# Attention computed a whole batch ahead, with transposed scores packed next to W1

## The chip, the cores and the metric

One core of one Trainium2 chip. The time is the device time of one execution in microseconds (us); a kernel's number is the median of its runs. The profile's span runs from the first to the last instruction and is about 1.8 us shorter than that time. "Fast runs" are those not in a disturbed state; a single run of a one-core program has the state "unknown".

The engines go by the profile's names: PE does the matmuls (PEld its weight loads), DVE is the vector engine, ACT the scalar engine, POOL is GpSimd, and SP does nothing here but issue DMAs. A small q (SPq) marks an engine's queue. PSUM is the memory that matmuls write, in banks. A hole is a time in which PE stands idle.

## The reference

Cross attention between x (8 batches, 8 heads, 512 tokens, 64 wide) and a state of 32 rows per head, in both directions, and then a two-layer network with SiLU (512 to 2048 to 512) over the result:

```
scores  = x @ state^T / 8        ; a  = softmax(scores)  ; xread = a  @ state     # 512 rows per head
scores2 = state @ x^T / 8        ; a2 = softmax(scores2) ; sread = a2 @ x         # 32 rows per head
y = concat(xread, sread)         ; h = y @ w_in          ; out = (h * sigmoid(h)) @ w_out
```

## The kernel before

The kernel folds the state into the first weight: for each batch, W1 = state @ w_in (its own matrix for each batch), so the hidden layer is W1^T times the attention weights a. A batch is 32 first-layer matmuls (`h`, from W1 and the transposed weights aT) and 64 second-layer ones (`o`), all 128x128 by 128x512, and the attention of the next batch, n = b + 1, is done in between. A pair (tt, ft) counts the second-layer matmuls: token tile tt of 4, hidden tile ft of 16.

```
def load_x(b, ...):                 # 1 MB, from GpSimd's queue (POOL)
    nc.gpsimd.dma_start(x_f[b % 2]..., x[b]...)
def transpose_x(b):                 # x^T by one DMA transpose of 512 KB, from the SP queue
    nc.sync.dma_start_transpose(xT[b], x_nat[b])
def scores(b, hg): ...              # 8 matmuls 128x128 by 128x64, into one of four rotating PSUM banks
def exps(b, hg):   ...              # one exp of 128x512 on ACT
def norm(b, hg, ...): ...           # sum, reciprocal (DVE), multiply (hg 0 on POOL, hg 1 on DVE)
def transpose_a(b, hg):             # aT by one DMA transpose of 128 KB, from the SP queue
    nc.sync.dma_start_transpose(aT[b][:, hg], an[b, hg])
...
# in the loop over batches, tiles tt and hidden tiles ft; n = b + 1
if at == (0, NFT - lead):  scores(n, 0); scores(n, 1); exps(n, 0); exps(n, 1)
if at == (1, 0):
    for hg in range(2):
        norm(n, hg, ...); transpose_a(n, hg)
    for c in range(4):     cast_x(n + 1, nc.gpsimd, c, 1)     # four casts on POOL
    load_x(n + 2)
if at == (2, 4):           sread(n); W1 first half            # takes all four rotating banks
if at == (3, 4):           W1 second half
if at == (3, 8):           transpose_x(n + 1)
```

The softmax here doesn't subtract the row's maximum and nothing guards it: scores larger than these inputs give would overflow.

## Time and profile before

| | before |
|---|---|
| time, median of 3 runs (lowest to highest) | 218.76 us (218.46 to 219.66) |
| span of the profiled run | 217.0 us |
| PE busy | 208.1 us (96%) |
| ACT, DVE, POOL busy | 142.5, 78.5, 42.0 us |
| one steady batch | 22.92 us |

The matmul stream (PE) is the bound: no other engine is busy for more than 73% of a steady batch, so what counts is the work of PE and whether something that PE needs arrives late. The lines that show this are in the prediction (in brackets, how long the engine was idle before and what ended that). One more view belongs here, because the result turns on it: the order of events on POOL and in the SP queue at (1, 0) of the loop over batch 4 (start, length, engine, line, operation, operands; in brackets, how long the engine was idle before and what ended that). First POOL, then SP:

```profile
122.34 1.04 POOL L327 TENSOR_TENSOR an<-exp_nat,rc 128x512 bf16<-128x512 bf16 x1 [18.30 <-ACT exp_nat L313]
123.33 2.74 POOL L153 CAST x_nat<-x_f 128x512 bf16<-128x512 f32 x4
126.03 0.93 POOL L106 DMA_DIRECT2D x_f<-in_x_dram  x1
```

```profile
123.41 2.50 SPq L337 DMA_TRANSPOSE aT<-an  x2
```

The two transposes of the weights leave at 123.41 and, one issue later, about 124.7; the casts keep the load of the next x back until 126.03.

### The profile page before, as it was taken

How to read it: one execution, taken by the hardware profiler on the slowest of the kernel's cores; microseconds unless marked ns; L12 is line 12 of the kernel's file. 1: busy time of each engine (PE TensorE's matmuls, PEld its weight loads, DVE VectorE, ACT ScalarE, POOL GpSimd, SP SyncE). 2: the span in 40 equal slices, each digit the busy share in tenths (PEclk: the TensorE clock that was granted, in tenths of full speed). 3: DMA queues.
4: the chain of work that ended last, by engine and by line, in shares of the span. 5: the costliest groups of instructions: out<-in, count | busy, mean ns of one | idle time of the engine just before them, and what ended most of it. 6: DMA issues, size and time to landing. Idle time of an engine off the chain costs nothing.

```text
span 217.0 us, 3946 instructions
## 1 busy us (share of the span) xinstructions
PE 208.1 (96%) x1579; PEld 98.0 (45%) x1605; DVE 78.5 (36%) x176; ACT 142.5 (66%) x243; POOL 42.0 (19%) x65
## 2 busy tenths in 40 slices
PE   7799999999999999999999989999999999999993
PEld 2433344444444444444444434444444444466652
DVE  4733248354642263206420632245222735200011
ACT  3765678799387956696669847893879566634410
POOL 8582004301600080006100440015000100000000
PEclk9999999999999999999999999999999999999999
DMA  5999999701497038802890199113510321011112
GB/s 191 186 204 207 220 340 300 227 37 51 111 211 183 0 108 259 174 3 75 232 201 34 54 155 285 50 51 102 146 51 0 102 102 48 0 48 51 48 48 97
DMA packets 33522, 27.09 MB, mean 125 GB/s; under 512 B 21344, under 2 KB 27360, under 8 KB 33504
## 3 DMA queue, kind: packets, MB, share of 16 engines
q1 hardware_dynamic: 26384, 14.95, 26.1%
q0 software_dynamic: 6976, 11.83, 24.0%
q8 instruction: 12, 0.20, 0.4%
q10 hardware_dynamic: 144, 0.07, 0.1%
q14 instruction: 6, 0.05, 0.1%
HBM read 17.43 MB, written 8.91 MB: 121 GB/s over the span
## 4 chain that ended last, share of the span: by engine, by line
PE 82%; issue 10%; DVE 2%; DMA 2%; POOL 2%; SPq 1%; POOLq 0%
PE o L485 43%; PE h L445 23%; PE ps_w L412 4%; PE h L464 3%; DMA aT<-an 2%; PE ps_busy L159 2%; PE o_half L507 2%; PE ps_sc L299 2%; PE o_a L485 1%; PE ps_sr L364 1%; POOL an L327 1%; DVE W L153 1%; PE ps_xt L245 1%; PE ps_at L344 1%; SPq L337 1%
## 5 line engine op out<-in xcount | busy, mean ns | idle before, releaser
L485 PE MATMUL o<-w_out_sb,g 128*128 128x512 bf16 x494 | 132.8, 380 | 1.9 <-issue 1.1
L477 ACT ACTIVATE g<-h 128x512 bf16<-128x512 f32 (+1 forms) x145 | 82.1, 571 | 35.7 <-PE h L445 21.4
L485 PEld LDWEIGHTS <-g 128*128 128x128 bf16 x528 | 49.8, 98 | 60.1 <-issue 7.0
L445 PE MATMUL h<-aT,W 128*128 128x512 bf16 x250 | 74.5, 379 | 0.7 <-DMA aT<-an 0.4
L153 DVE COPY o_sb<-o 128x512 f32<-128x512 f32 x17 | 11.6, 690 | 82.6 <-PE o L485 82.6
L445 PEld LDWEIGHTS <-W 128*128 128x128 bf16 x256 | 24.7, 97 | 31.3 <-issue 1.8
L153 DVE CAST W<-ps_w 128x512 bf16<-128x512 f32 (+1 forms) x31 | 20.5, 679 | 34.8 <-PE ps_w L412 34.8
L327 POOL TENSOR_TENSOR an<-exp_nat,rc 128x512 bf16<-128x512 bf16 (+1 forms) x9 | 9.1, 1014 | 112.2 <-DVE rc L325 56.7
L151 ACT ACTIVATE W<-ps_w 128x512 bf16<-128x512 f32 (+1 forms) x35 | 18.7, 577 | 7.6 <-PE ps_w L412 7.5
L151 ACT ACTIVATE o_sb<-o 128x512 f32<-128x512 f32 x15 | 8.9, 596 | 18.7 <-issue 9.1
L153 POOL CAST x_nat<-x_f 128x512 bf16<-128x512 f32 x24 | 16.0, 702 | 0.0
L412 PE MATMUL ps_w<-w_in_sb,stT 64*32 64x512 bf16 (+1 forms) x264 | 11.5, 376 | 0.0
L324 DVE TENSOR_REDUCE rs<-exp_nat 128x16 f32<-128x512 bf16 (+1 forms) x17 | 10.7, 630 | 1.4 <-ACT exp_nat L313 0.5
L106 POOL DMA_DIRECT2D x_f<-in_x_dram x8 | 7.0, 886 | 14.4 <-DVE x_rows L153 12.5
L313 ACT ACTIVATE exp_nat<-ps_sc 128x512 bf16<-128x512 f32 (+1 forms) x17 | 9.0, 570 | 1.3 <-PE ps_sc L299 1.2
L464 PE MATMUL h<-xmT,w_in_sb 128*128 128x256 bf16 x64 | 9.6, 273 | 0.1
L464 PEld LDWEIGHTS <-w_in_sb 128*128 128x128 bf16 x64 | 6.3, 98 | 3.9
L313 ACT ACT_TABLE_LOAD x6 | 7.7, 1283 | 0.1
L636 ACT ACT_TABLE_LOAD x6 | 7.7, 1283 | 0.1
L159 PE MATMUL ps_busy<-busy 128*128 128x512 bf16 x15 | 5.7, 497 | 1.4 <-DVE warm L166 1.2
L327 DVE TENSOR_TENSOR an<-exp_nat,rc 128x512 bf16<-128x512 bf16 (+1 forms) x8 | 6.7, 831 | 0.3
L299 PEld LDWEIGHTS <-xT 128*128 128x128 bf16 x128 | 4.9, 98 | 2.9 <-DVE xT L153 1.0
(59 smaller groups left out, 90.1 us busy)
## 6 DMA issues: line engine op xcount, KB each, us to landing
out_dram<-o_sb SPq DMA_DIRECT2D x33, 256.0 KB, 2.5
x_f<-in_x_dram POOLq DMA_DIRECT2D x6, 1024.0 KB, 7.9
w_in_sb<-in_moe_w_in_dram POOLq DMA_DIRECT2D x3, 512.0 KB, 10.1
w_out_sb<-in_moe_w_out_dram POOLq DMA_DIRECT2D x3, 512.0 KB, 11.8
x_f<-in_x_dram SPq DMA_DIRECT2D x2, 512.0 KB, 4.8
x_f<-in_x_dram POOLq DMA_DIRECT2D x2, 512.0 KB, 16.6
w_in_sb<-in_moe_w_in_dram POOLq DMA_DIRECT2D x2, 256.0 KB, 7.5
w_out_sb<-in_moe_w_out_dram POOLq DMA_DIRECT2D x2, 256.0 KB, 7.9
```

Source lines behind the costliest of these rows:

```text
L151: nc.scalar.activation(dst, src, func=COPY, bias=0.0)
L153: eng.tensor_copy(dst, src)
L159: nc.tensor.matmul(ps[:], busy[:, 0:128], busy[:], start=True, stop=True, skip_group_check=True)
L299: nc.tensor.matmul(sc_ps[hg][-1][:, c % m, ds(2 * j, 2), :], xT[b][:, c, 2 * hg + j, :], stT[:, b, 2 * hg + j, :, :], start=True, stop=Tru ...
L313: nc.scalar.activation(e[:, ds(n * i, n)], ps[:], func=EXP, bias=0.0, scale=SCALE)
L324: nc.vector.tensor_reduce(rs[:, ds(c, nr)], e[:, ds(c, nr)], axis=AX, op=ADD)
L327: eng.tensor_tensor(a[:, ds(c, n)], e[:, ds(c, n)], rc[:, ds(c, n)].to_broadcast([128, n, 4, NS]), op=MULT,)
L412: nc.tensor.matmul(pss[f, hg][ds(32 * s, 32), 0:n], stT[ds(r, 64), b, h // 2, s % 2, :], w_in_sb[ds(r, 64), h // 2, ds(f, n)], start=True, ...
L445: nc.tensor.matmul(h_ps[k][:], W1[b][:, hg, ds(128 * ft, 128)], aT[b][:, hg, :, :], start=(hg == 0), stop=(hg == 1), skip_group_check=True,)
L464: nc.tensor.matmul(ps[:, 0:256], w_in_sb[:, kt, ds(128 * ft, 128)], xmT[:, :, kt].rearrange("p t n b -> p t (n b)"), start=(kt == 0), stop ...
L477: nc.scalar.activation(g[:, ds(i, m)], ps[:, ds(i, m)], func=SILU, bias=0.0)
L485: nc.tensor.matmul(outs[tt][:], gt[b * NFT + ft][:, ds(128 * tt, 128)], w_out_sb[:, ft, :], start=(ft == 0), stop=(ft == NFT - 1), skip_gr ...
```

## The change

Its intent: from batch 3 on, the attention of batch m = b + 2 is done while batch b's network runs, so that its long chain (exp, transpose, normalize, transpose) has a whole batch of slack. Scores are computed transposed, in the 64x32 tile group that W1 already uses, next to W1's matmuls and without a mode switch of their own; the exponentials and their normalized form are each transposed by one DMA. Batch 2 still goes the old way, so the loop over batch 1 does both. The core of the diff (warm-up activations, PSUM tags and the old branch are cut; they do not matter here):

```
+    def scores_t(b):
+        scT_ps[0] = psO.tile(..., tag="o1");  scT_ps[1] = psH.tile(..., tag="h1")
+        for s in range(4):
+            for hg in range(2):                       # 8 matmuls, 64x32 tiles, 512 columns
+                nc.tensor.matmul(scT_ps[hg][ds(32 * s, 32), :], stT[ds(r, 64), b, h // 2, s % 2, :],
+                                 xT[b][ds(r, 64), :, h // 2, :], ..., tile_position=(r, 32 * s))
+    def exps_t(b):   # two exps on ACT, then one DMA transpose e <- eT of 256 KB
+    def norm_t(b):   # sum, reciprocal, multiply, then one DMA transpose aT <- a of 256 KB
 ...
             pe_transpose_a(1, 1, nc.vector)
-            for c in range(4):
-                cast_x(2, nc.gpsimd, c, 1)
+            for i in (2, 3):
+                for c in range(4):
+                    cast_x(i, nc.gpsimd, c, 1)        # batch 3's casts moved ahead
 ...
                     if at == (1, 0):                  # (for b == 1)
                         for hg in range(2):
-                            norm(n, hg, ...); transpose_a(n, hg)
-                        if n + 1 < B:
-                            for c in range(4):
-                                cast_x(n + 1, nc.gpsimd, c, 1)
-                        if n + 2 < B:
-                            load_x(n + 2)
+                            norm(2, hg, ...); transpose_a(2, hg)
+                        load_x(4)                     # now directly behind norm
+                if b == 2 and at == (0, 4):
+                    transpose_x(4)
 ...
+                if n < B and at == (1, 4):            # was (2, 4)
+                    scores_t(m)
+                    pss = w1_mms(n, ...)
+                    sread((0, 1, 2) if b == 1 else (n,))
+                    exps_t(m)
 ...
+                    if at == (3, 0):
+                        norm_t(m)
+                        if b == 1:
+                            for c in range(4):
+                                cast_x(4, nc.gpsimd, c, 1)
+                        if m + 2 < B:
+                            load_x(m + 2)
 ...
+                    if at == (2, 8):                  # was (3, 4)
                         w1_chunks(n, (2, 3), both)
 ...
-        copy(nc.vector, o[:], ps[:, 0 : DM // 2])     # last copy of all
+        for i, eng in enumerate((nc.vector, nc.scalar)):
+            copy(eng, o[:, ds(DM // 4 * i, DM // 4)], ps[:, ds(DM // 4 * i, DM // 4)])
```

More of the change, by code (lines that the diff above doesn't have):

```diff
@@ L61 @@
     wpool = ctx.enter_context(tc.tile_pool(name="wpool", bufs=2))
+    tpool = ctx.enter_context(tc.tile_pool(name="tpool", bufs=2))
+    e2pool = ctx.enter_context(tc.tile_pool(name="e2pool", bufs=3))
     gpool = ctx.enter_context(tc.tile_pool(name="gpool", bufs=28))
     opool = ctx.enter_context(tc.tile_pool(name="opool", bufs=4))
-    psO = ctx.enter_context(tc.tile_pool(name="psO", bufs=2, space=bass.MemoryType.PSUM))
+    psO = ctx.enter_context(tc.tile_pool(name="psO", bufs=1, space=bass.MemoryType.PSUM))
     psH = ctx.enter_context(tc.tile_pool(name="psH", bufs=2, space=bass.MemoryType.PSUM))
@@ L120, in padded, with spread_x @@
         )[:, :, :, 0:128]
+    def spread_x(b):
+        copy(nc.vector, padded(b), x_nat[b][:])
     def cast_x(b, eng, c0=0, nc_=4, h0=0, nh=H):
@@ L170 @@
     )
-    nc.scalar.activation(warm[:], warm[:], func=EXP, bias=0.0)
+    nc.scalar.activation(warm[:], busy[:, 0:1], func=EXP, bias=0.0)
     for hg in range(2):
@@ L259 @@
     cast_x(0, nc.scalar, 2, 2, 0, 4)
-    new_o = lambda sh, dt, nm: psO.tile(sh, dt, tag="o", name=nm)
+    o_tags = ["o0", "o1"]
+    new_o = lambda sh, dt, nm: psO.tile(sh, dt, tag=o_tags.pop(), name=nm)
     cast_x(0, nc.scalar, 2, 2, 4, 4)
@@ L313, in exps @@
             nc.scalar.activation(e[:, ds(n * i, n)], ps[:], func=EXP, bias=0.0, scale=SCALE)
+    scT_ps = {}
+    eT = {}
+    def scores_t(b):
+        scT_ps[0] = psO.tile([128, 512], FP32, tag="o1", name="ps_scT")
+        scT_ps[1] = psH.tile([128, 512], FP32, tag="h1", name="ps_scT")
+        for s in range(4):
+            for hg in range(2):
+                h = HEAD_OF_SLOT[hg][s]
+                r = 64 * (h % 2)
+                nc.tensor.matmul(
+                    scT_ps[hg][ds(32 * s, 32), :],
+                    stT[ds(r, 64), b, h // 2, s % 2, :],
+                    xT[b][ds(r, 64), :, h // 2, :],
+                    start=True,
+                    stop=True,
+                    tile_position=(r, 32 * s),
+                    skip_group_check=True,
+                )
+    def exps_t(b):
+        t = tpool.tile([128, 2, 512], BF16, tag="eT", name="eT")
+        e = e2pool.tile([128, 2, 4, 4, NS], BF16, tag="e2", name="e2")
+        for hg in range(2):
+            nc.scalar.activation(t[:, hg], scT_ps[hg][:], func=EXP, bias=0.0, scale=SCALE)
+            exp_nat[b, hg] = e[:, hg]
+        nc.sync.dma_start_transpose(
+            e.rearrange("p g c s n -> p (g c) (s n)"), t.rearrange("q g t -> q (g t)")
+        )
+        e2[b] = e
+    e2 = {}
+    def norm_t(b):
+        rs = att.tile([128, 2, 4, 4, 1], FP32, tag="rs2", name="rs2")
+        rc = att.tile([128, 2, 4, 4, 1], FP32, tag="rcn", name="rcn")
+        a = tpool.tile([128, 2, 4, 4, NS], BF16, tag="an2", name="an2")
+        nc.vector.tensor_reduce(rs[:], e2[b][:], axis=AX, op=ADD)
+        nc.vector.reciprocal(rc[:], rs[:])
+        for hg, eng in enumerate((nc.gpsimd, nc.vector)):
+            eng.tensor_tensor(
+                a[:, hg], e2[b][:, hg], rc[:, hg].to_broadcast([128, 4, 4, NS]), op=MULT
+            )
+        aT[b] = att.tile([128, 2, 4, 128], BF16, tag="aT", name="aT")
+        nc.sync.dma_start_transpose(
+            aT[b].rearrange("q g c p -> q (g c) p"), a.rearrange("p g c s n -> p (g c s n)")
+        )
     an = {}
@@ L483, in G2 @@
             else:
-                outs[tt] = psO.tile([128, DM], FP32, tag="o", name="o")
+                i = (tt + (b > 0)) % 2 if tt < 3 else 0
+                outs[tt] = psO.tile([128, DM], FP32, tag=f"o{i}", name="o")
         nc.tensor.matmul(
@@ L538 @@
     w1_cols(0, [(0, 256)], (nc.scalar, nc.scalar))
-    nc.scalar.activation(warm[:], warm[:], func=SILU, bias=0.0)
+    nc.scalar.activation(warm[:], busy[:, 0:1], func=SILU, bias=0.0)
     load_w_in(1024)
@@ L549 @@
         ones_beside_x(i, nc.gpsimd)
-    keep_busy(4, psO, "o")
+    keep_busy(4, psO, "o0")
     pe_transpose_a(0, 0, nc.vector)
-    keep_busy(1, psO, "o")
+    keep_busy(1, psO, "o0")
     pe_transpose_a(0, 1, nc.vector)
@@ L577 @@
         if ft == 14:
-            nc.scalar.activation(warm[:], warm[:], func=EXP, bias=0.0)
+            nc.scalar.activation(warm[:], busy[:, 0:1], func=EXP, bias=0.0)
             pe_transpose_x(1, 0, 1, engs=(nc.vector,))
@@ L596 @@
     store(0, 2, nc.scalar)
-    nc.scalar.activation(warm[:], warm[:], func=SILU, bias=0.0)
+    nc.scalar.activation(warm[:], busy[:, 0:1], func=SILU, bias=0.0)
     store(0, 1, nc.vector)
@@ L617 @@
         n = b + 1
+        m = n + 1
         lead = 4 if b == 1 else 6
@@ L623 @@
                     upto(NFT * b + min(lead + ft, NFT))
-                if b == 1 and at == (0, 1):
-                    transpose_state()
-                    for u in range(2):
-                        evict_state(u, nc.vector)
                 if b == B - 1 and at in ((0, 4), (0, 8)):
                     place_xm(at[1] // 8, nc.vector)
-                if n < B:
-                    if at == (0, NFT - lead):
-                        scores(n, 0)
-                        scores(n, 1)
-                        exps(n, 0)
-                        exps(n, 1)
-                        nc.scalar.activation(warm[:], warm[:], func=SILU, bias=0.0)
+                if b == 1:
+                    if at == (0, 1):
+                        transpose_x(3)
+                        transpose_state()
+                        for u in range(2):
+                            evict_state(u, nc.vector)
+                    if at == (0, 4):
+                        spread_x(2)
+                    if at == (0, NFT - lead):
+                        for hg in range(2):
+                            scores(2, hg)
+                        for hg in range(2):
+                            exps(2, hg)
@@ L637 @@
                     if at == (1, 0):
                         for hg in range(2):
-                            norm(n, hg, (((nc.gpsimd, nc.vector)[hg], 0, 4),))
-                            transpose_a(n, hg)
-                        if n + 1 < B:
-                            for c in range(4):
-                                cast_x(n + 1, nc.gpsimd, c, 1)
-                        if n + 2 < B:
-                            load_x(n + 2)
-                    if at == (3, 8):
-                        if n + 1 < B:
-                            transpose_x(n + 1)
@@ L649 @@
-                    if at == (0, 4):
-                        copy(nc.vector, padded(n), x_nat[n][:])
-                    if at == (2, 4):
-                        if b == 1:
-                            sread((0, 1))
-                        sread((n,))
-                        pss = w1_mms(n, [(0, 512), (512, 512)])
-                        w1_out(n, [(0, 512)], both, pss)
-                        for m in (0, 1, 2) if b == 1 else (n,):
-                            sread_out(m)
-                        w1_out(n, [(512, 512)], both, pss)
@@ L660 @@
-                    if at == (3, 4):
+                            norm(2, hg, (((nc.gpsimd, nc.vector)[hg], 0, 4),))
+                            transpose_a(2, hg)
+                        load_x(4)
+                elif at == (0, NFT - lead) and m < B:
+                    nc.scalar.activation(warm[:], busy[:, 0:1], func=EXP, bias=0.0)
+                if b == 2 and at == (0, 4):
+                    transpose_x(4)
+                if b > 1 and m + 1 < B:
+                    if at == (1, 0):
+                        for c in range(4):
+                            cast_x(m + 1, nc.gpsimd, c, 1)
+                    if at == (2, 10):
+                        transpose_x(m + 1)
@@ new lines @@
+                if n < B and at == (1, 4):
+                    if m < B:
+                        scores_t(m)
+                    pss = w1_mms(n, [(0, 512), (512, 512)])
+                    sread((0, 1, 2) if b == 1 else (n,))
+                    if m < B:
+                        exps_t(m)
+                        nc.scalar.activation(warm[:], busy[:, 0:1], func=SILU, bias=0.0)
+                    w1_out(n, [(0, 512)], both, pss)
+                    for i in (0, 1, 2) if b == 1 else (n,):
+                        sread_out(i)
+                    w1_out(n, [(512, 512)], both, pss)
@@ L661 @@
+                if m < B:
+                    if at == (2, 0):
+                        spread_x(m)
+                    if at == (3, 0):
+                        norm_t(m)
+                        if b == 1:
+                            for c in range(4):
+                                cast_x(4, nc.gpsimd, c, 1)
+                        if m + 2 < B:
+                            load_x(m + 2)
+                if n < B:
+                    if at == (2, 8):
                         w1_chunks(n, (2, 3), both)
```

## The prediction

> **What bounds the kernel now.** I read the page's busy shares first, then the stretches of one batch each, then the instructions in order of time inside one batch, and last the chain of waits at the two places where a batch was longer than its neighbours.
>
> ```profile
> PE 208.1 (96%) x1579; PEld 98.0 (45%) x1605; DVE 78.5 (36%) x176; ACT 142.5 (66%) x243; POOL 42.0 (19%) x65
> PEclk9999999999999999999999999999999999999999
> ...
> 73.24:96.15 22.91, 22.65 (x173) 10.26 (x176) 8.04 (x17) 16.66 (x28) 4.61 (x6) 1.00 0.51 129
> 96.15:119.10 22.95, 22.65 (x173) 10.26 (x176) 8.03 (x17) 16.70 (x28) 4.61 (x6) 1.00 0.54 128
> 119.10:142.54 23.44, 22.81 (x173) 10.24 (x176) 8.03 (x17) 16.62 (x28) 4.61 (x6) 1.00 0.53 126
> 142.54:165.46 22.92, 22.65 (x173) 10.26 (x176) 8.03 (x17) 16.67 (x28) 3.73 (x5) 1.00 0.29 83
> 165.46:187.90 22.44, 22.18 (x158) 9.77 (x160) 10.42 (x24) 16.24 (x27) 1.05 (x1) 1.00 0.19 61
> ```
>
> The first column after the stretch is its length, then the busy time of PE, PEld, DVE, ACT and POOL. PE is busy in 22.65 of about 22.92 us at full clock; nothing else passes 73%. So the kernel ends when the matmul stream ends, and only two things can change its time: the work in that stream, and holes in it. Each stretch begins right after the scores of a batch. The last one contains no scores, as there is no batch 8, and is 22.92 - 22.44 = 0.48 us shorter: a direct reading of what one batch's scores cost end to end. One stretch, 119.10 to 142.54, is 0.52 us longer than the others.
>
> The order in time of one batch (start, length, line, operands, count):
>
> ```profile
> 141.91 0.63 PE L299 MATMUL ps_sc<-stT,xT 128*128 128x64 bf16 x16
> 142.59 5.56 PE L485 MATMUL o<-w_out_sb,g 128*128 128x512 bf16 x25
> 148.08 0.43 PE L364 MATMUL ps_sr<-x_rows,exp_nat 128*32 128x65 bf16 x32
> 148.44 0.62 PE L412 MATMUL ps_w<-w_in_sb,stT 64*32 64x512 bf16 x16
> 149.23 2.75 PE L485 MATMUL o<-w_out_sb,g 128*128 128x512 bf16 x12 [0.16 <-issue]
> ...
> 153.42 0.63 PE L412 MATMUL ps_w<-w_in_sb,stT 64*32 64x512 bf16 x16
> 153.98 0.39 PE L485 MATMUL o<-w_out_sb,g 128*128 128x512 bf16 x1
> ```
>
> The program has 26 second-layer matmuls between scores and state read but 25 records, so one is missing just ahead of 142.59; the scores took 0.47 us, as the chain of waits also says (PE ps_sc x16, 0.47). The state read takes 148.44 - 148.08 = 0.36 us, W1's 16 matmuls 153.98 - 153.42 = 0.56 us. With pairs of full matmuls at 0.43 us in the chain (0.216 each), a batch is 96 x 0.216 = 20.7, scores 0.47, state read with W1 and the switch ahead of them 1.01, second W1 group with its switch 0.65: 22.83 of 22.92. There is no unused tenth in this loop.
>
> Two more readings, both used below:
>
> ```profile
> 28.49 0.41 PE L412 MATMUL ps_w<-w_in_sb,stT 64*32 64x512 bf16 x8
> 28.83 0.61 PE L485 MATMUL o<-w_out_sb,g 128*128 128x512 bf16 x2
> ...
> 50.97 0.69 DVE L153 COPY o_sb<-o 128x512 f32<-128x512 f32 x1 [4.69 <-PE o L485]
> 51.55 1.08 ACT L313 ACTIVATE exp_nat<-ps_sc 128x512 bf16<-128x512 f32 x2
> ...
> 128.34 0.38 PE L445 MATMUL h<-aT,W 128*128 128x512 bf16 x1
> ...
> 129.12 0.38 PE L445 MATMUL h<-aT,W 128*128 128x512 bf16 x1 [0.41 <-DMA aT<-an]
> ```
>
> Eight matmuls in the 64x32 grouping take 28.83 - 28.49 = 0.34 us, sixteen 0.56: eight more, inside a group that is there anyway, cost 0.22. And the long stretch is the one where the transposed attention weights landed late: 129.12 - 128.34 less one matmul of 0.22 is 0.56.
>
> **What the Trainium skill says.** "TensorE: Matmul & The Clock Gate", section "Wait — 56ns, not 53.3ns?", gives 215.7 ns from start to start at 512 columns; the trace's 0.43 us per pair agrees. "TensorEngine Tiling (Array Packing)", section "Key Properties", says that a change of tiling mode drains the array, while tiles of one mode run independently. The trace agrees: about 0.09 us of lost start time ahead of 153.42 (153.11 plus one matmul is 153.33), and the 0.34 and 0.56 above. "ScalarE: Activation LUTs", section "What ACT_TABLE_LOAD costs", gives about 1283 ns for a load; the rows here show 1283. "DMA: Bandwidth & Descriptors", section "Rules for kernel authors", advises to issue a DMA early and wait late; that is the intent of this change, and the 4.4 us of the one late transpose, against a median of 2.3, shows what too short a lead costs.
>
> **The change part by part.**
>
> Scores removed: batches 3 to 7 lose sixteen 128x64 matmuls with as many weight loads of 98 ns. 5 x 0.47 = 2.35 us off the stream.
>
> Transposed scores added: eight 64x512 matmuls for each of these batches, placed next to W1 in the same mode, so no new switch. 5 x 0.22 = 1.10 us on the stream. The state read moves behind W1, which leaves the number of switches as it was. I take that as nothing. Net -1.25.
>
> Exp and normalization: two exps of 128x512 as before (0.60 each), the same sum, reciprocal and multiply work on DVE and POOL in one piece. One more DMA transpose of 256 KB per batch; by the 2.3 us of 128 KB and the median 5.6 us of 512 KB I estimate 3.4 us for it. From the exps to the first use of the attention weights there is now a whole batch, some 30 us, against a chain of about 0.2 + 1.2 + 3.4 + 2.6 + 3.4 = 11 us. So the wait at 129 goes: -0.52. Table loads fall from six pairs in the loop to five; ACT is at 73%, so they are worth nothing.
>
> PSUM: the transposed scores borrow a bank of the second layer's output and one of the hidden pair. The first is free when DVE has copied the first output tile. The copy ended 1.1 us after that tile's last matmul began (143.45 to 144.56), and the new scores would start 1.2 us after it: just free, at most 0.1 us lost. The other is free since all hidden tiles are activated by then.
>
> Batch 1's loop, the transition, carries both methods. The exps of batch 2 still end at 52.63. W1 of batch 2 now comes four second-layer matmuls into the second token tile, at about 51.95 after the new scores, and takes all four rotating banks. Two of them hold batch 2's scores until its exps end. The first eight matmuls go (to 52.2), the rest wait until about 52.7: +0.5 us. Then DVE has batch 2's norm (to 54.9 as before), a W1 copy 0.7, three state-read outputs of 0.93 each and another W1 copy, which ends near 59.1; the second W1 group, now eight matmuls into the third token tile at 58.4, needs that bank half way through: another +0.45. Together +0.95 us, once.
>
> Tail: the last copy of 128x256 (0.42 on DVE) is shared. From 424 at 256 and 690 ns at 512 columns, 128 columns are about 0.29: -0.13.
>
> Sum: -2.35 + 1.10 - 0.52 + 0.95 - 0.13 = -0.95 us, so 218.76 becomes 217.8.
>
> **The rivals.** *No transition loss*: bank order or DVE order is kinder than I count, and the gain is the whole 1.9 us: 216.9. For it: both waits are half a microsecond on chains that I added up by hand. *A late transpose*: batch 4's x loads only after batch 2's norm (about 55.3), lands some 8 us later, is cast by POOL for 2.7 us behind batch 3's multiply, and its transpose is behind the last store of batch 1 in the SP queue, so it leaves near 68.8 and lands 3.8 to 7.3 us later; its scores want it near 75.9. Mostly in time; at worst 0.5 to 1 us more: 218.8. *Transposes in the way*: one DMA transpose more per batch delays stores on the same queue until output buffers run out. Against it: DMA is at about half in these stretches and the queue has roughly 12 of 22.7 us of issuing to do. If it came, each batch would lose up to 1 us and the time would be 221 or more. *A gain beyond 2%* would need 4.4 us; all scores of these five batches are 2.35, so nothing in the profile can give it.
>
> **Range and chances.** The sure terms are the scores (-1.25) and the late weights (-0.5); the unsure one is the transition (0 to +1.5, perhaps with batch 4's lateness). Repeats of the kernel before differ by 1.2 us (218.46 to 219.66). I give 217.8, 8 in 10 between 216.4 and 219.2; faster by over 2% 0.02, within 2% 0.95, slower by over 2% 0.03.
>
> **What would show it.** Stretches of steady batches should be 22.6 to 22.7 us. The eight new matmuls and W1's sixteen together should take about 0.78 us before the state read, against 0.56 for W1. No matmul should wait on aT from batch 3 on. In batch 1's loop PE should show one hole near 52 us ended by ACT's exp and one near 59 ended by a DVE copy of W. I am wrong if steady stretches stay at 22.9 (then a mode switch or the borrowed bank costs what the scores gave), or if holes ended by DMA or POOL appear.

## The result, and the profile after

The changed kernel is slower: median 222.06 us (221.42 to 222.58, 4 runs) against 218.87 us for the kernel before in the same rounds, ratio 1.014 (95% interval 1.0097 to 1.0183). It is within 2% and well outside my range of 216.4 to 219.2. A ratio is the mean time of one kernel's fast runs over the mean of the other's of the same rounds, so it is not quite the ratio of the medians. The profiled run took 222.43 us, span 220.7 us: 3.7 us more than the span before.

The steady loop did what it should. The page's first line and the stretches, cut right behind the state read of each batch (columns as in the prediction: length, then busy time of PE, PEld, DVE, ACT, POOL):

```profile
PE 207.1 (94%) x1539; PEld 96.5 (44%) x1565; DVE 75.7 (34%) x166; ACT 140.8 (64%) x246; POOL 42.2 (19%) x65
```

```profile
49.84:81.95 32.11, 26.79 (x299) 12.07 (x300) 13.23 (x33) 20.45 (x34) 8.84 (x12) 1.00 0.72 152
81.95:104.57 22.62, 22.36 (x165) 9.91 (x168) 7.52 (x16) 16.75 (x29) 4.70 (x6) 1.00 0.61 139
104.57:127.19 22.62, 22.36 (x165) 9.92 (x168) 7.59 (x16) 16.75 (x29) 4.70 (x6) 1.00 0.64 141
127.19:149.81 22.62, 22.36 (x165) 9.93 (x168) 7.58 (x16) 16.75 (x29) 1.49 (x1) 1.00 0.42 96
149.81:172.22 22.41, 22.14 (x158) 9.80 (x161) 7.60 (x16) 15.02 (x27) 1.50 (x1) 1.00 0.28 69
```

Three equal batches of 22.62 us, where they were 22.92 and once 23.44. The last one has no transposed scores in it, and is 22.62 - 22.41 = 0.21 us shorter: that is what they cost. But in the first stretch, 49.84 to 81.95, PE is idle for 32.11 - 26.79 = 5.3 us. The matmuls there, in order of time:

```profile
51.66 0.41 PE L331 MATMUL ps_scT<-xT,stT 64*32 64x512 bf16 x8
51.89 1.14 PE L466 MATMUL ps_w<-w_in_sb,stT 64*32 64x512 bf16 x16
52.96 0.96 PE L418 MATMUL ps_sr<-x_rows,exp_nat 128*32 128x65 bf16 x96
...
58.93 0.41 PE L466 MATMUL ps_w<-w_in_sb,stT 64*32 64x512 bf16 x8 [0.25 <-DVE W L158]
59.27 2.12 PE L540 MATMUL o<-w_out_sb,g 128*128 128x512 bf16 x9
64.10 0.60 PE L499 MATMUL h<-aT,W 128*128 128x512 bf16 x2 [2.71 <-DMA aT<-an]
...
80.59 0.41 PE L331 MATMUL ps_scT<-xT,stT 64*32 64x512 bf16 x8 [1.82 <-DMA xT<-x_nat]
80.81 0.61 PE L466 MATMUL ps_w<-w_in_sb,stT 64*32 64x512 bf16 x16
81.36 0.43 PE L418 MATMUL ps_sr<-x_rows,e 128*32 128x65 bf16 x32
```

The two large holes are named in the brackets: 2.71 us for the transposed weights of batch 2 (hole 1), and 1.82 us for the transposed x of batch 4 (hole 2). Both are DMA transposes that were issued early enough and landed late. The queues at the two places, first POOL, then SP:

```profile
54.25 0.93 POOL L108 DMA_DIRECT2D x_f<-in_x_dram  x1
...
68.39 2.27 POOL L158 CAST x_nat<-x_f 128x512 bf16<-128x512 f32 x4
70.62 0.93 POOL L108 DMA_DIRECT2D x_f<-in_x_dram  x1
```

```profile
54.34 3.23 SPq L391 DMA_TRANSPOSE aT<-an  x2
...
71.29 6.27 SPq L143 DMA_TRANSPOSE xT<-x_nat  x1
```

Each late transpose leaves within 0.7 us of a load of 1 MB. Batch 3's casts are no longer between `norm` and the load, so the load starts with the weights' transposes and not 2.6 us after them. At the second place one event releases both: the end of batch 4's casts at 70.66 frees POOL for the next load and lets the transpose of what was just cast go, behind one store. Hence theory A: **a load from another queue that starts together with DMA transposes holds them back until it has landed itself.** The rival, theory B: the transposes that the change adds (of the exponentials, and the state reads' earlier ones) delay one another on the SP queue, and the load is innocent.

The packets of the trace support A before any experiment. Per microsecond of the changed kernel, on the clock of the lines above, the KB that were started and the mean and longest time of one packet, transposes (SP queue, packets of 256 bytes) against the load (POOL queue, 4096 bytes):

```
us        transposes: KB, mean / longest ns      load: KB, mean / longest ns
56         64.8,   26 /  546                      60,  2494 / 2967
57          1.2,   18 /   18                      24,   452 / 1912
58          1.5,   19 /   22                      64,  1074 / 2015
59          3.2,   19 /   22                      36,   757 / 1285
60          9.8,  168 / 2946                     240,   188 /  198
61          0                                    300,   188 /  193
62         11.0,   18 /   21                     300,   188 /  193
63        245.5,   20 /   79                       0
```

(The row of 60 contains two transpose packets of 2946 ns. By 57, 121 KB of the two transposes' 256 KB had started.) From 57 to 60 hardly anything moves in either queue: many load packets take one to three microseconds, not 0.19. Then the load runs at full speed, and only when it is through (its last packet ends at 62.97) do the transposes go on, with the usual 20 ns per packet. At hole 2 the picture is alike but not as sharp: from 72 to 77 the transpose starts 0 to 13 KB per microsecond, then 99 and 123 KB beside the load's last packets.

The kernel before has such collisions too, at transposes for which nobody waits: that of the state read (`xs`) took 7.4, 7.8 and 6.1 us to landing where a load of x was under way (issued at 81.26, 104.17 and 128.07), and 2.3 us where none was (150.57). Its one long batch is another matter. There the second transpose of the weights took 4.4 us; but the load left 1.3 us behind it, as in the three batches before, where that transpose took 2.3 to 2.4 us. Its slow packets, up to 1979 ns, start at 126.4, and the load's first packet only at 127.7. What this batch alone has in these microseconds is a packet of 16 KB in the queue that the profile calls `instruction`, from 125.82 on, 1776 ns long. So it is not shown that the load made this transpose late, and the `instruction` packet is a suspect.

### The profile page after: what moved, and what is told of

It reads as the page before. It is cut to its first block, busy times and chain, and to the rows that moved or that the text cites.

```text
span 220.7 us, 3845 instructions
## 1 busy us (share of the span) xinstructions
PE 207.1 (94%) x1539; PEld 96.5 (44%) x1565; DVE 75.7 (34%) x166; ACT 140.8 (64%) x246; POOL 42.2 (19%) x65
## 4 chain that ended last, share of the span: by engine, by line
PE 78%; DMA 13%; POOL 2%; DVE 2%; issue 1%; ACT 1%; SPq 0%; POOLq 0%
PE o L540 44%; PE h L499 22%; DMA w_in_sb<-in_moe_w_in_dram 5%; DMA aT<-an 4%; DMA xT<-x_nat 4%; PE ps_w L466 4%; PE h L518 3%; PE o_half L562 2%; PE o_a L540 1%; DVE W L158 1%; PE ps_sr L418 1%; POOL w_in_sb L149 1%; PE ps_scT L331 1%; POOL w_out_sb L152 1%; ACT L319 1%
## 5 line engine op out<-in xcount | busy, mean ns | idle before, releaser
L499 PE MATMUL h<-aT,W 128*128 128x512 bf16 x244 | 73.1, 379 | 3.0 <-DMA aT<-an 2.7
L158 DVE CAST W<-ps_w 128x512 bf16<-128x512 f32 (+1 forms) x31 | 20.5, 677 | 29.1 <-PE ps_w L466 29.1
L361 POOL TENSOR_TENSOR an<-e,rcn 128x512 bf16<-128x512 bf16 x5 | 7.6, 1523 | 59.5 <-DVE rcn L359 59.5
L158 POOL CAST x_nat<-x_f 128x512 bf16<-128x512 f32 x24 | 13.7, 606 | 25.8 <-DMA x_f<-in_x_dram 25.8
L466 PE MATMUL ps_w<-w_in_sb,stT 64*32 64x512 bf16 (+1 forms) x264 | 12.0, 375 | 0.5 <-DVE W L158 0.2
L345 ACT ACTIVATE eT<-ps_scT 128x512 bf16<-128x512 f32 x10 | 5.4, 598 | 3.5 <-PE ps_scT L331 3.5
L358 DVE TENSOR_REDUCE rs<-e 128x32 f32<-128x1024 bf16 x5 | 6.1, 1210 | 4.5 <-DMA e<-eT 4.5
L466 PEld LDWEIGHTS <-stT 64*32 64x32 bf16 x264 | 3.6, 89 | 8.4 <-issue 6.2
L381 POOL TENSOR_TENSOR an<-exp_nat,rc 128x512 bf16<-128x512 bf16 (+1 forms) x4 | 3.9, 982 | 15.7 <-DVE rc L379 15.7
L540 PE MATMUL o_a<-w_out_sb,g 128*128 128x512 bf16 x15 | 5.5, 379 | 0.0
```

What stands on the lines that cost most here:

```text
L158: eng.tensor_copy(dst, src)
L358: nc.vector.tensor_reduce(rs[:], e2[b][:], axis=AX, op=ADD)
L361: eng.tensor_tensor(a[:, hg], e2[b][:, hg], rc[:, hg].to_broadcast([128, 4, 4, NS]), op=MULT)
L466: nc.tensor.matmul(pss[f, hg][ds(32 * s, 32), 0:n], stT[ds(r, 64), b, h // 2, s % 2, :], w_in_sb[ds(r, 64), h // 2, ds(f, n)], start=True, ...
L499: nc.tensor.matmul(h_ps[k][:], W1[b][:, hg, ds(128 * ft, 128)], aT[b][:, hg, :, :], start=(hg == 0), stop=(hg == 1), skip_group_check=True,)
L540: nc.tensor.matmul(outs[tt][:], gt[b * NFT + ft][:, ds(128 * tt, 128)], w_out_sb[:, ft, :], start=(ft == 0), stop=(ft == NFT - 1), skip_gr ...
```

## The experiments

Each is a small edit of one of the two kernels; some build on an earlier one, and then it is said. "Hole 1" and "hole 2" are those above.

### The kernel before, with the load ahead of the casts

```
                     if at == (1, 0):
                         for hg in range(2): norm(...); transpose_a(n, hg)
+                        if n + 2 < B:
+                            load_x(n + 2)
                         if n + 1 < B:
                             for c in range(4): cast_x(n + 1, nc.gpsimd, c, 1)
-                        if n + 2 < B:
-                            load_x(n + 2)
```

> The kernel before with one reordering: in each batch the load of the x two batches ahead is issued ahead of the four casts on GpSimd, not behind them, so it starts with the two transposes of the attention weights instead of 2.7 us after them. Theory A (an x load of 1 MB that starts with DMA transposes holds them back until it has landed itself, 8 to 9 us): the transposes land some 9 us after issue, not 2.3, in batches 1 to 4; the first-layer matmuls, which want them about 5 us after issue, stall about 4 us in each of the four, so about 16 us more, near 235 us. Theory B (the extra DMA transposes of the changed kernel delay each other on their queue; the load is innocent): there are no extra transposes here, so 218.9 us as before.

Measured: correct, 239.76 us (236.75 to 240.38, 4 runs, of which the last is slow and left out of the ratio) against 218.71; ratio 1.0901 (1.0812 to 1.099). This is the heaviest evidence: two lines exchanged, same work, no new transposes, and 21 us more. The waits of PE, and the first hole in order of time:

```profile
PE h L445 <- DMA aT<-an: 13.6, 5, 3.9
```

```profile
62.27 0.38 PE L445 MATMUL h<-aT,W 128*128 128x512 bf16 x1 [2.56 <-DMA aT<-an]
63.96 0.59 PE L445 MATMUL h<-aT,W 128*128 128x512 bf16 x1 [1.32 <-DMA aT<-an]
64.34 1.06 PE L485 MATMUL o<-w_out_sb,g 128*128 128x512 bf16 x2
65.19 1.06 PE L445 MATMUL h<-aT,W 128*128 128x512 bf16 x2
```

The transposes land a median of 8.0 us after issue in that batch, where it was 2.3. Theory B predicts 218.9 and is out for this kernel. The waits make 13.6 us and not 16, and something else makes the rest: after a hole of about 4 us a pair of matmuls takes 1.06 us and not 0.6. The granted clock over the whole run is 0.964, and (1 - 0.964) x 237.5 = 8.5 us. 13.6 + 8.5 = 22 us against the 20.5 us by which the span grew: the two together account for it, roughly, as a low clock partly falls into the holes. In the trace's clock records the low clock comes as half speed for 3.41 us at a time, five such periods in this run, two of them in a row. The Trainium skill, "TensorE: Matmul & The Clock Gate", section "Why this matters for your kernels", advises to leave no gap of more than about 3 us between matmul bursts. Here the holes of 2.56 and 1.32 us, with one matmul between, were enough.

### The changed kernel without batch 4's load

```
                             norm(2, hg, ...); transpose_a(2, hg)
-                        load_x(4)
```

> The changed kernel without the load of batch 4's x (batch 4 is computed on stale data, so a wrong result on purpose). Theory A: the weights of batch 2 land about 3 us after issue, the hole of 2.7 us near 61 us goes, the hole ahead of batch 4's transposed scores stays at 1 to 2 us as the load of batch 5's x still meets that transpose; about 219.4 us. Theory B: the extra transposes are all there, so the hole of 2.7 us stays; 222 us.

Measured: wrong result (relative error 0.032); 217.67 us, span 215.9, one run. Hole 1 is gone, with every transpose of the changed kernel in place; the weights land in a median of 2.7 us.

```profile
59.27 2.12 PE L540 MATMUL o<-w_out_sb,g 128*128 128x512 bf16 x9
61.22 0.59 PE L499 MATMUL h<-aT,W 128*128 128x512 bf16 x2
```

My number of 219.4 was too high since hole 2 went as well: without hole 1 batch 4's casts are done at 66.2 and not 70.7, the transpose of its x leaves at 68.41, collides with the next load (6.8 us to landing), and is still there just ahead of its use at 75.81. Hole 2 is thus partly a consequence of hole 1.

### The changed kernel without batch 5's load

```
-                        if m + 2 < B:
+                        if m + 2 < B and b > 1:
                             load_x(m + 2)
```

> The changed kernel without the load of batch 5's x (a wrong result on purpose). Theory A: the transpose of batch 4's x lands 4 to 5 us after issue, not 9.3, and the hole of 1.8 us ahead of batch 4's transposed scores goes; the hole of 2.7 us near 61 us stays; about 220.2 us. Theory B: both holes stay; 222 us.

Measured: wrong result; 218.68 us, span 216.9, one run. Hole 2 is gone, and no transpose of an x in this run takes more than 4.5 us to land, where batch 4's had taken 9.3. Hole 1 is there but only 0.80 us long, not 2.7, although the two kernels do not differ up to that point. So the length of the collision varies from run to run, and 220.2 was a miss for that reason. In this run the load's packets were slow for one microsecond only, not four.

### The changed kernel with the other transposes of batch 1 put off

```
+        def go():
             nc.sync.dma_start_transpose(e..., t...)        # and the same for the three xs transposes
+        if b == 3: held.append(go)
+        else:      go()
...
+                    if b == 1 and at == (3, 2):
+                        for f in held: f()                  # norm_t(3) follows at (3, 3)
```

> The changed kernel with the load kept, but in batch 1 the transpose of the exponentials and the three of the state reads are put off until the hidden matmuls of the last token tile have begun, so that behind the two transposes of batch 2's weights nothing follows on the queue. Theory A: the hole near 61 us stays, 2 to 3 us. Theory B: it goes. In both the later normalization of batch 3 can make the hole ahead of batch 4's scores larger, so the time itself decides nothing: 222 to 226 us under A, 219 to 223 under B.

Measured: correct, 225.17 us, one run. Until 62.53 nothing but stores follows the two weight transposes (54.66 and 57.10) on the queue. By then these were long overdue; they landed at 65.42 and 65.68, right behind the load at 65.20, and hole 1 is the longest of all:

```profile
65.47 1.01 PE L510 MATMUL h<-aT,W 128*128 128x512 bf16 x2 [3.76 <-DMA aT<-an]
```

Theory B falls: the load is what it takes, and the added transposes are not needed for it. (Hole 2 is 1.73 us here.)

### Both loads early

```
                     if at == (0, 1):
                         transpose_x(3)
+                        load_x_sp(4); load_x_sp(5)         # the same loads, from the SP queue
-                        load_x(4)                          # at (1, 0)
-                        if m + 2 < B:           load_x(m + 2)
+                        if m + 2 < B and b > 1: load_x(m + 2)
```

> The changed kernel, correct, with the loads of batch 4's and 5's x moved: both are issued by the SP queue behind the transpose of batch 3's x, in the stretch after 45 us in which the DMA engines had been idle, so that no x load meets the transposes of batch 2's weights or of batch 4's x. Theory A (load and transpose collide): both holes go, 2.7 and 1.8 us, and what is left is the sum of my prediction without its tail term, so 217.3 to 218.0 us. Theory C (the wait at those places is made by the new order of the queues, whatever the load does): at least one hole of over 1 us stays, 219 us or more.

Measured: correct, 218.14 us (218.03 to 218.55, 4 runs), span 216.3, ratio to the kernel before 0.9981 (0.9959 to 1.0003). Both holes are gone, and theory C with them. (The weights still took 4.2 and 3.4 us, with no load in flight; the run has an `instruction` packet at 56.51 and transpose packets of up to 934 ns from 57.3 on.) The median is 0.1 us above my range; the span is what my sum gives with the tail as measured (217.0 - 0.95 + 0.31 = 216.4). So the change, freed of the collisions, is worth what I had worked out: almost nothing.

### Early loads, batch 1's block later, last copy whole

```
  (as above, and)
-                if n < B and at == (1, 4):
+                if n < B and at == ((1, 10) if b == 1 else (1, 4)):
-                    if at == (2, 8):
+                    if at == ((3, 4) if b == 1 else (2, 8)):
-        for i, eng in enumerate((nc.vector, nc.scalar)): ...
+        copy(nc.vector, o[:], ps[:, 0 : DM // 2])
```

> As the run with both loads early, and in batch 1 the transposed scores, W1 and state read come six second-layer matmuls later and the second W1 group twelve later, so that the banks are free when they are wanted (0.5 and 0.45 us by the trace of the changed kernel), and the last copy is whole on DVE again (0.60 us in two serial halves against 0.42). Expected: the run with both loads early less 1.0 to 1.2 us, so 216.2 to 216.9 us, which is faster than both kernels by 1 to 1.3% and 2.3 to 2.6%. If the two bank waits were really something else, it is only 0.2 us below the run with early loads.

Measured: correct, 217.2 us (217.1 to 217.26, 5 runs), ratio to the kernel before 0.9931 (0.9916 to 0.9946). It beats both kernels: the one before by 0.7%, the changed one by (222.06 - 217.2) / 222.06 = 2.2%. It gained 0.94 us over the run before, 0.06 less than the least I expected. The block in batch 1:

```profile
53.28 0.41 PE L334 MATMUL ps_scT<-xT,stT 64*32 64x512 bf16 x8
53.51 0.61 PE L469 MATMUL ps_w<-w_in_sb,stT 64*32 64x512 bf16 x16
54.05 0.96 PE L421 MATMUL ps_sr<-x_rows,exp_nat 128*32 128x65 bf16 x96
```

W1's sixteen matmuls now take 54.05 - 53.51 = 0.54 us, where they took 1.07 (51.89 to 52.96). From the end of batch 2's scores to the end of batch 3's state read the stretch is 26.37 us against 27.34 with early loads alone: 0.97 us, the two bank waits exactly. In this profile the part of the program ahead of batch 2's scores, which the edit does not touch, was 0.3 us longer (50.16 against 49.83), which is the size of what is missing, though one profile each does not show that the timed runs differ by it.

### Only batch 4's load on the SP queue, at its place

```
                             norm(2, hg, ...); transpose_a(2, hg)
-                        load_x(4)
+                        load_x_sp(4)                       # behind the two transposes, same queue
```

> The changed kernel with the load of batch 4's x at the same place, but issued from the SP queue right behind the two transposes of batch 2's weights instead of from GpSimd beside them. The bytes and the moment are the same within 2 us; only the queue differs, and with it whether packets of the load and of these transposes interleave. If interleaving of the two queues is the cause: the weights land about 3 us after issue and the hole near 61 us goes; about 217.5 to 219.5 us. If any load in those microseconds is enough: the hole stays, 1 us or more.

Measured: correct, 232.94 us, one run; far from either number. Hole 1 is gone (the weights land in a median of 2.7 us; their last packet starts at 58.1 and the load's first at 58.8). But the second collision, batch 5's load from POOL with the transpose of batch 4's x, has become the worst:

```profile
87.98 0.63 PE L334 MATMUL ps_scT<-xT,stT 64*32 64x512 bf16 x8 [12.07 <-DMA xT<-x_nat]
```

```profile
x_f<-in_x_dram POOLq DMA_DIRECT2D x1, 1024.0 KB, 17.6
out_dram<-o_sb SPq DMA_DIRECT2D x1, 256.0 KB, 12.6
xT<-x_nat SPq DMA_TRANSPOSE x1, 17.7
```

Load (issued at 70.13) and transpose (70.21) started within 0.1 us of each other, and both took over 17 us: from 73 on they crawl side by side, with at most 39 KB of the transpose and 128 KB of the load in any microsecond. In the kernel before the loads take a median of 7.9 and such a transpose 3.8 to 7.3. I had not reckoned with what the edit does to the second place. As a test of hole 1 it says what was asked; as a warning it says more: the price of a collision is not bounded by the length of the load alone.

### The changed kernel with the last copy whole on DVE

```
-        for i, eng in enumerate((nc.vector, nc.scalar)): ...
+        copy(nc.vector, o[:], ps[:, 0 : DM // 2])
```

> The changed kernel with the last copies whole on DVE as before. Expected from the trace: from the last matmul to the end 0.15 to 0.2 us shorter than in the changed kernel, as its two half copies ran one after the other (0.29 + 0.03 + 0.28 against 0.42). It is at the same time a second look at the hole near 61 us, which was 2.7 in one run and 0.8 and 3.8 us in two others that should not differ there: it should lie between those.

Measured: correct, 222.05 us, span 220.2, one run. From the first matmul of the last group to the end of the last copy it takes 217.23 - 213.12 = 4.11 us; the changed kernel took 217.66 - 213.36 = 4.30. The tail of the changed kernel, in order of time:

```profile
213.36 3.66 PE L562 MATMUL o_half<-w_out_sb,g 128*128 128x256 bf16 x32
...
217.06 0.29 DVE L158 COPY o_half<-o_half 128x128 f32<-128x128 f32 x1 [1.46 <-PE o_half L562]
217.38 0.28 ACT L156 ACTIVATE o_half<-o_half 128x128 f32<-128x128 f32 x1 [1.47 <-DVE o_half L158]
```

ACT's half waits for DVE's, so the split costs 0.19 us and does not save 0.13. Hole 1 in this run is 3.04 us, and the stretch after it shows the clock (third number from the right):

```profile
64.44:68.00 3.56, 3.34 (x10) 1.40 (x11) 2.27 (x3) 1.20 (x2) 0.75 (x1) 0.62 0.68 202
```

At a granted clock of 0.62, PE needs about 1.3 us more for the next matmuls (the third pair of first-layer matmuls starts 3.03 us after the hole, in the changed kernel's profile 1.73). That puts off the use of batch 4's x as well: its transpose lands at 80.29, and its scores begin at 80.34, where the changed kernel wanted them at 78.77. Hence no hole 2 here. In these two runs a hole 1 is paid for by a hole 2 or by a low clock, and the total is the same (222.05 against a median of 222.06 us).

### A control: only batch 5's load early

```
                         transpose_x(3)
+                        load_x_on(nc.sync, 5)
...                      # load_x(4) stays on POOL at (1, 0)
-                        if m + 2 < B:
+                        if m + 2 < B and b > 1:
                             load_x(m + 2)
```

> A control for the next run: the changed kernel with only the load of batch 5's x moved early, so that only the first collision, batch 4's load from GpSimd beside the transposes of batch 2's weights, is left. Expected: a hole near 61 us of 0.8 to 3.8 us, as in the four looks so far; no hole ahead of batch 4's transposed scores; 218.5 to 221.5 us.

Measured: correct, 219.55 us, span 217.8, one run: hole 1 of 1.20 us, weights 7.7 us to landing, no hole 2. As expected.

### Batch 4's load from the ACT queue

```
  (the control, and)
-                        load_x(4)
...
                         nc.scalar.activation(warm[:], ..., func=SILU)
+                        if b == 1:
+                            load_x_on(nc.scalar, 4)
```

> As the control, but batch 4's load at the same place is issued from the ACT queue (behind the exps and the table load, near 55 us, while the transposes of 54.3 to 57.5 are under way) and not from GpSimd. If it is the meeting of two queues on the DMA engines that holds the transposes, they still land 6 us or more after issue and a hole of 0.5 to 4 us stays. If it is something of the GpSimd queue[...], the transposes land within 4 us and the hole goes; about 218 us.

Measured: correct, 218.07 us, span 216.3, one run, no hole; the weights landed in a median of 5.4 us. **Inconclusive**: the load was issued at 52.33, ahead of the exps and the table load queued on ACT (they ended at 54.9), so 831 of its 1024 packets had started when the transposes' first packet did, at 56.7.

### The same, held back until the transposes leave

```
+                        nc.vector.memset(x_f[0][:, 0, 0, 0:1], 0.0)   # behind DVE's part of norm(2)
...
+                            load_x_on(nc.scalar, 4)                   # now waits for it
```

> The run before it with the load on the ACT queue again, as there the load was issued at 52.3 us, ahead of the work queued on ACT, and was nearly done when the transposes began. Now it waits for a one-element memset by DVE behind its part of batch 2's normalization, so it starts near 55 us, within a microsecond of the transposes, as GpSimd's did. If the meeting of a load and transposes on the DMA engines holds them: they land 6 us or more after issue and a hole of 0.5 to 4 us comes near 61 us; 218.5 to 221.5. If only loads from GpSimd do that: they land within 4 us and there is no hole; about 218 us.

Measured: correct, 218.26 us, span 216.5, one run. The load was issued at 54.90. The profile of 54 to 66:

```profile
x_f<-in_x_dram ACTq DMA_DIRECT2D x1, 1024.0 KB, 6.1
```

The weights took a median of 6.5 us (2.3 in the kernel before), and in the packets the transposes stand nearly still from 57 to 60 and go on at 60, as the load's last packets pass (its last one ends at 60.5). So the holding back is not peculiar to GpSimd's queue: a load from ACT's queue does it too. The hole I gave as 0.5 to 4 us did not come (0.1 at most), because this load took only 6.1 us, where GpSimd's took 7.5 to 10.6 at this place; PE wants the weights at 61.2, and the transposes were through by then.

### Both loads at their places, both on the SP queue

```
-                        load_x(4)
+                        load_x_on(nc.sync, 4)
...
-                            load_x(m + 2)
+                            load_x_on(nc.sync, 5)          # for b == 1
```

> The changed kernel with both loads left at their places in the program but issued from the SP queue, each behind the transposes issued before it: batch 4's behind those of batch 2's weights, batch 5's behind that of batch 3's weights and ahead of that of batch 4's x. If order within one queue is what the transposes need: no hole at either place, 217.5 to 218.8 us, against 232.9 us where only batch 4's load was moved. If batch 4's x still comes late because it is queued behind 1 MB: a hole of up to 2 us, 220 us.

Measured: correct, 222.81 us, span 221.0, one run. No hole 1 (weights in 2.7 us), and the 17 us of the collision are gone, but the second branch of the expectation holds: batch 4's transpose stands in the queue behind 1 MB, its issue alone takes 5.77 us, and hole 2 is 2.76 us, followed by 3.41 us at half clock. Order in one queue protects what is ahead, and delays what is behind.

## Why the prediction was wrong

By the steps of its sum, in us, measured from the two profiled runs:

| step | predicted | measured |
|---|---|---|
| scores out, transposed scores in, five batches | -1.25 | -1.35 (5 x (0.48 - 0.21)) |
| late weights in the 119 to 142 stretch gone | -0.52 | -0.52 |
| two bank waits in batch 1's loop | +0.95 | +0.97 (1.07 - 0.55, and 59.27 - 58.27 less 0.55) |
| tail | -0.13 | +0.18 |
| weights of batch 2 late (hole 1) | not in the sum | +2.71 |
| x of batch 4 late (hole 2) | rival, "at worst 0.5 to 1" | +1.82 |
| sum | -0.95 | +3.81 (spans: +3.7) |

**What was right.** PE as the bound, the price of both kinds of scores, both waits for banks (each within 0.05 us, and removed by the run that moves the block), and that the whole gain is below 1%. The run with early loads confirms the sum by itself.

**The step that failed** is the time that a DMA transpose takes to land, which was carried over from the kernel before. The sum lets batch 2's weights land as there (2.3 us); they took 9.7 and 7.9 us, and PE waited 2.71 us. Batch 4's x was given 3.8 to 7.3 us; it took 9.3, and PE waited 1.82 us. The text's own sign of being wrong, "holes ended by DMA", came up twice. Three places led there. First, the late transpose near 129 was read as a matter of lead: "shows what too short a lead costs". Its lead, 3.9 us from issue to need, was that of the other batches; it took 4.4 us in place of 2.3, and why stays open (see the packets above). From that reading followed that more lead cures everything, and batch 2's weights, which keep their old lead, were not looked at: the sum has no term for them. Second, the load was counted as something that may itself be late ("loads only after batch 2's norm (about 55.3), lands some 8 us later"), never as something that makes others late, though the text says when it starts, and the transposes start at the same time. The page's 6.1 us for `xs` was a hint: without a load in flight it is 2.3. Third, "Transposes in the way" was argued away with "DMA is at about half in these stretches". An average of busy shares says nothing of two particular transfers that start together. The diff had the cause in plain sight: the casts that moved had been keeping load and transposes apart.

The rival "a late transpose" named the right place for hole 2 and sized it from landing times of 3.8 to 7.3 us in a kernel where a transpose rarely met a load from its start. It was 9.3, and its issue was at 71.29, not 68.8, since hole 1 had moved everything.

**The tail** failed on an assumption: that two engines copying the two halves of a tile run side by side. In both copies ACT starts 0.03 us after DVE ends.

In the steady loop the collision still happens: the weights of batches 4 and 5, whose transposes leave 0.1 us after a load, take 9.1 and 9.8 us, those of batches 6 and 7, without a load, 3.1. But there the change has its batch of slack, and nobody waits. The change makes transposes robust from batch 3 on, and exposes them in the transition, where the slack is not yet there.

**What stays open.** Hole 1 was 2.71, 0.80, 3.76, 3.04 and 1.20 us in five kernels that do not differ in the load, its queue or these two transposes. In all five the weights land 0.2 to 0.6 us after the load, and the hole is the load's own time to landing (9.45, 7.53, 10.63, 9.78 and 7.96 us) less 6.7 to 6.9 us. So the question is why the load's time varies, and what inside the DMA engines stops the transposes. The packets show that a load's first packets are as stuck as the transposes, and no run here says which waits for which.

A second disturber was not tested. In the changed kernel and all its variants but one a 16 KB `instruction` packet starts between 54.8 and 57.7, near the weights' transposes. It does not make hole 1 alone: the run without batch 4's load has one at 54.92, and its weights land in 3.1 and 2.4 us. Nor does the collision need it: in the steady loop of the changed kernel the weights issued at 91.08 took 9.1 us with none between 81.72 and 100.61. But it may be what made the weights take 4.4 us in the kernel before and 4.2 us with both loads early. No run varied it.

## What to carry to other kernels

When an edit moves work on an engine that also issues DMA, ask what that work was delaying: four casts that nobody waited for kept a 1 MB load away from two transposes, and issuing the load ahead of them cost 21 us in the plainest test. Place bulk loads where no transfer with a deadline is in flight, or behind it on its own queue, and then check what is queued behind the load. Check the transition batches of a software pipeline by their own timeline, as they have the new traffic and not yet the new slack.

## What the Trainium skill lacked or had wrong

- "DMA: Bandwidth & Descriptors", section "Rules for kernel authors", says that a transpose next to ordinary DMAs needs nothing. That row is about correct data, and all runs here with collisions that should be correct are. It lacks the price in time: beside a 1 MB load from another queue, a pair of transposes of 128 KB took 6.5 to 9.7 us (medians) in place of 2.3 to 2.7, and one of 512 KB took 17.7 in place of 3.8 to 7.3.
- The same page, section "Queues, rings and completion order", has each DMA engine take turns between the queues, packet by packet. That is not what the trace shows at hole 1: the transposes' packets of 256 bytes moved 0 to 11 KB per microsecond from 57 until the load was through, 0 and 11 KB in the two microseconds in which the load moved 300 KB each.
- The same page has no number for what such a collision costs the load: many of its first 4096-byte packets took 1 to 3 us, then 0.19.
- "TensorE: Matmul & The Clock Gate", section "Back-to-back issue gap", gives about 131 ns per matmul at 512 columns as the sustained rate in a stream with weight loads. Here a long stream of such matmuls, each with its own weights, runs at 216 ns, the figure which the same page gives for the single case.
- On clock and holes that page agrees with the runs in the main: holes of 3.04 and 3.76 us came with a period of 3.41 us at half clock, which began up to 0.7 us before their end, and that of 12.07 us with 13.65 us. Near its limit of about 3 us it is not the length alone that decides: a hole of 2.76 us was followed by one, a hole of 2.71 us was not.
- "TensorEngine Tiling (Array Packing)", section "Key Properties", names the drain at a mode switch but gives no size: about 0.09 us ahead of a 64x32 group here. Eight more matmuls in a group that exists cost 0.21 to 0.22 us.
- No page says in so many words that a DMA issued from ACT can leave ahead of activations that come before it in the program: it left at 52.33, with a table load and two exps ahead of it still to run until 54.9.
